# First batch of a fused attention kernel: v loaded ahead of w_out, six of thirteen pieces split, second batch's first keys scored early

## The chip, the cores and the metric

The kernel runs on one core of a Trainium2 chip. The core has five engines with a queue each: PE (TensorE: matrix products into the accumulators, PSUM), DVE (VectorE), ACT (ScalarE), POOL (GpSimd) and SP (SyncE, which here only issues transfers). Each engine takes its instructions strictly in the order in which they were written, so one that waits holds up all behind it. The metric is device time in microseconds (us); a lower one is better. All positions below, such as "at 62.38", are us from the start of the profiled span.

## The reference, cut to what matters

```python
def _attn_ref(q, k, v, agents):            # 4 batches, 12480 tokens, 128 channels, 49 agents
    def sm(a, b):
        s = (a @ b.transpose(0, 2, 1)) / sqrt(128)
        e = np.exp(s - s.max(-1, keepdims=True))
        return e / (e.sum(-1, keepdims=True) + 1e-09)
    agent_v = sm(agents, k) @ v            # needs all keys and values of the batch
    return sm(q, agents) @ agent_v

x = _attn_ref(...).reshape(49920, 128)
out = np.maximum(x @ w_in, 0.0) ** 2 @ w_out       # 128 -> 2048 -> 128
```

w_in and w_out arrive as 64-bit floats and are turned into 32-bit floats on the chip, bit by bit.

## The kernel before

Tokens are cut into 52 groups of 960, thirteen to a batch; keys and values of a batch come in thirteen pieces as well. A batch needs, ahead of its first tokens, its agent values, folded into the first weight matrix (`w_make`: 98 rows of products, a high and a low part, of which 49 rows of `w_lo` are spread over the partitions by small transfers into `w_a` and `w_b`). Once that is there, a group is sixteen steps of: `mm1` (two steps at a time), `relu` and `square` on ACT, `high` and `low` on DVE (a number is split into a rounded high part and the rest, so that PE can take both at its fast 32-bit rate), and `mm2`, four steps later, in the same order on PE (`LAG = 4`). While one batch runs, the next one's keys, values and weights are made in the gaps by a planner (`plan_batch`, `plan_tokens`, `chain`), which hands out one slot per step and engine.

For the first batch nothing runs in which to hide that, so the first 100 us are a preamble written out by hand: a list of `at(time, function)` calls, sorted by time, sets the order on every queue. Its parts, in order:

- keys (`k_load`, `k_scores`, `k_copy`, `k_pmax`) with the conversion of three of the four parts of w_in (`win_make`, seven DVE instructions each) in between, then the maximum over keys (`k_max`, steps 0 to 5, a ping-pong of DVE and PE);
- the v stage, for each of thirteen pieces: `sub0` on DVE, `k_exp` on ACT, then `v_acc_whole` on PE: eight products of 32-bit operands that are not split, accumulated in one PSUM bank over all pieces. Between them on DVE stand the fourth part of w_in and three of the four parts of w_out (`wo_make`, seven instructions each, then `wo_split` on ACT and POOL);
- `v_sum_whole`, `a_final` (PE and DVE by turns), `w_make` for columns 0 and 1 of four, the fourth `wo_make`, and the first steps. The other two `w_make` follow among them; `mm1` of steps 8 and 9 is the first to need the third.

Transfers stand on SP in the order of their `at` times: v piece by piece with a part of w_out after every third and the second group's q after the tenth. Keys, queries and v share a pool of six buffers (`io`), so that a transfer starts when an earlier tile has been read; the raw parts of w_in and w_out have four buffers of another pool (`ew`). Two of the four spread transfers of the first `w_b` are issued by ACT, the others by SP.

Of the kernel before, what the change touches and what calls it, by code (L numbers as in the profile page):

```python
# [25 lines left out]
def agent_attention_relu2_kernel(ctx: ExitStack, tc: tile.TileContext, qT, kT, v, agT, w_in, w_out, outT):  # L26
# [41 lines left out]

    raws = {}

    def raw_load(t, src):
        raw = ew.tile([P, PW, 2], U32, name="raw", tag="gl")
# [29 lines left out]

    def wo_make(t, step):
        if step == 0:
            wo[t] = ew.tile([P, PW], F32, name="wo_f", tag="gh")
            cv["o"] = to_f32(raws.pop((t, False)), wo[t])
        cv["o"][step]()

    def wo_split(t, step):
# [30 lines left out]

    def piece(n):
        return sk[:, n * G:(n + 1) * G, :]
# [50 lines left out]
            nc.sync.dma_start(out=vts[n][:, halves[h]], in_=v[b, :, n * G + h * H:n * G + (h + 1) * H, :])  # L195

    def v_hi(n, h):
        nc.scalar.copy(vss[n % 2][:, halves[h], :C], vts[n][:, halves[h], :C])

    def v_lo(n, h, eng=nc.vector):  # L200
        vs = vss[n % 2][:, halves[h]]
        eng.tensor_tensor(out=vs[:, :, C + 2:], in0=vts[n][:, halves[h], :C], in1=vs[:, :, :C].bitcast(F32), op=ALU.subtract)  # L202

    def v_acc(n):
        vs, pe = vss[n % 2], pes.pop(n)
        vts.pop(n)
        pss["v", n] = bank()
        for c in range(G):
            nc.tensor.matmul(pss["v", n][:A2, :VW], pe[:, c, :], vs[:, c], start=c == 0, stop=c == G - 1)  # L209

    def v_acc_whole(n, ps):

        vt = vts.pop(n)
        for c in range(G):
            nc.tensor.matmul(ps[:A, :C + 1], piece(n)[:, c, :], vt[:, c, :C + 1], start=n == 0 and c == 0, stop=c == G - 1 and n == NS - 1)

    def v_sum_whole(ps):
        nc.vector.tensor_copy(acc[:A, :C + 1], ps[:A, :C + 1])

    def v_sum(n):  # L220
        ps = pss.pop(("v", n))[:A2, :VW]
        if n == 0:
            nc.vector.tensor_copy(acc, ps)
        else:
            nc.vector.tensor_tensor(acc, ps, acc, op=ALU.add)
# [235 lines left out]
    def plan_batch(b, base, span):  # L461

        d = (span - 46) / (2 * NS)
        for n in range(NS):
            t = n if b == 1 and n < AHEAD else base + int(n * d)
            first, end = chain(t, [("PE", k_scores, b, n), ("ACT", k_copy, n), ("DVE", k_pmax, n)])
            if b > 1 or n >= AHEAD:
                at(max(base, first - 8), k_load, b, n)
# [35 lines left out]
    at(Z + .2, q_load, 0)  # L504
    for n in range(NS):
        at(Z + .3 + n * .01, v_load, 0, n)
    at(Z + .395, q_load, 1)
    for n, x, src in ((0, .025, wi_bits), (1, .055, wi_bits), (2, .085, wi_bits), (3, .125, wi_bits),
                      (0, .325, wo_bits), (1, .355, wo_bits), (2, .385, wo_bits), (3, .415, wo_bits)):
        at(Z + x, raw_load, n, src)  # L510
    for n in range(NS):
        t = Z + 6 + KP * n
        at(t, k_scores, 0, n)
# [2 lines left out]
        at(t + 1.8, k_pmax, n)  # L516
    for x in range(7):
        for n in range(3):
            at(Z + 10 + 6 * n + .8 * x, win_make, n, x)
    t0 = Z + 6 + KP * NS  # L520
    at(t0, k_max, 0)
    for x in range(1, 6):
        at(t0 + .8 + .4 * x, k_max, x)
    at(t0 + .1, warm_up, 3)
# [6 lines left out]
    def sub0(n):  # L531
        k_sub(n, nc.vector, pss["m"][:CH, :A])

    for n in range(NS):
        t = t0 + 1.84 * n
        at(t, sub0, n)
        at(t + .5, k_exp, n)
        at(t + 2.4, v_acc_whole, n, vps)
    for x in range(7):
        at(t0 + 2 + .7 * x, win_make, 3, x)  # L540
        for n in range(3):
            at(t0 + 7 + 5 * n + .7 * x, wo_make, n, x)
    for n in range(3):
        for x in range(2):
            at(t0 + 13 + 5 * n + x, wo_split, n, x)
    for x, f in enumerate((q_exp, q_sum, q_inverse, q_norm, q_hi, q_lo)):
        at(t0 + 2 * x + 2.2, f, 0)
    at(t0 + 18, q_transpose, 0)
    for x in range(2):
        at(t0 + 18.1, q_copy, 0, x)  # L550
    at(t0 + 19, q_spread, 0)
    for n in range(AHEAD):
        at(t0 + 20 + .1 * n, k_load, 1, n)
    t += 4.2
    at(t, v_sum_whole, vps)
    at(t + .2, warm_up, 2)
    for x in range(4):
        at(t + .3 + (0, 1, 2, 2)[x], a_final, x)
    at(t + 1.5, warm_up, 4)
    for f in range(2):  # L560
        for x in range(4):
            at(t + 4 + .1 * x + .5 * f, w_make, 0, f, x)
    at(t + 5, warm_up, 3)
# [54 lines left out]
```

## Time and profile before

| | us |
|---|---|
| median of 3 runs | 2052.86 (2051.44 to 2054.33) |
| profiled execution, own time | 2051.45 |
| its span | 2049.7 |
| PE busy of it | 2028.1 (99%) |
| DVE, ACT, POOL busy | 1823.4, 1730.2, 230.8 |

The span is 1.75 us shorter than the execution's own time, and that execution is 1.4 us below the median. PE is busy in nearly all of it, but a share of the span says little here, since the change touches only the first 130 us. Those are read piece by piece: the chain of waits, the order in time of each engine, and narrow windows with the granted clock.

### The profile page before, as it was taken

The numbers are of one execution on the slowest core, as the hardware profiler recorded it, in microseconds if no ns is written. First come the engines' busy times: TensorE is split into PE (matmuls) and PEld (weight loads), VectorE is DVE, ScalarE is ACT, GpSimd is POOL, SyncE is SP. The second block draws the span as 40 slices with busy tenths as digits, with TensorE's granted clock in tenths as the row PEclk, the third lists the DMA queues.
The fourth block names the chain that finished last, engine by engine and source line by source line (L and its number), as shares of the span: only waits on it lengthen the run. The fifth ranks groups of instructions, "written<-read, shape, count | busy, mean of one in ns | idle before, by whom it ended". The sixth has DMA issues, their size and how long they took to land.

```text
span 2049.7 us, 30393 instructions
## 1 busy us (share of the span) xinstructions
PE 2028.1 (99%) x11010; PEld 1584.9 (77%) x11015; DVE 1823.4 (89%) x2274; ACT 1730.2 (84%) x2166; POOL 230.8 (11%) x196
## 2 busy tenths in 40 slices
PE   9899999999999999999999999999999999999999
PEld 8678877777778877777777878777777777777777
DVE  7678899999888889999998888999998888989897
ACT  2488889899888888999888888999888888889897
POOL 0100002221000001232100000122210000000000
PEclk9899999999999999999999999999999999999999
DMA  9322212211121212222112121122111111101010
GB/s 310 90 67 66 71 48 70 79 49 40 56 66 57 66 61 70 61 68 60 35 46 79 56 72 60 61 68 70 45 36 50 44 31 45 30 30 41 29 35 25
DMA packets 51446, 125.16 MB, mean 61 GB/s; under 512 B 7072, under 2 KB 16560, under 8 KB 51296
## 3 DMA queue, kind: packets, MB, share of 16 engines
q1 hardware_dynamic: 51198, 123.19, 19.4%
q8 instruction: 86, 1.41, 0.3%
q14 instruction: 64, 0.52, 0.1%
q10 hardware_dynamic: 98, 0.04, 0.0%
HBM read 81.37 MB, written 25.56 MB: 52 GB/s over the span
## 4 chain that ended last, share of the span: by engine, by line
PE 86%; DVE 8%; issue 4%; DMA 1%; ACT 1%; SPq 0%; ACTq 0%; DVEq 0%
PE out L378 51%; PE h L348 16%; PE h L351 8%; PE ps_att L154 3%; PE ps_att L285 3%; DVE gh L363 3%; DVE gl L367 2%; PE ps_att L322 1%; PE ps_att L209 1%; DVE vs L202 1%; DMA vt<-v 1%; PE ps_att L262 1%; PE h L154 0%; DVE ob L396 0%; PE out L495 0%
## 5 line engine op out<-in xcount | busy, mean ns | idle before, releaser
L367 DVE TENSOR_TENSOR gl<-g,gh 128x960 fp32r<-128x960 f32 x832 | 1015.8, 1221 | 30.6
L355 ACT ACTIVATE r<-h 128x960 f32<-128x960 f32 x832 | 764.4, 974 | 179.0 <-PE h L351 175.8
L359 ACT ACTIVATE g<-r 128x960 f32<-128x960 f32 x832 | 825.5, 1016 | 5.1 <-DVE gl L367 5.1
L378 PE MATMUL out<-gh,wo_hi 128*128 128x480 f32 x1664 | 689.6, 414 | 5.2 <-DVE ob L396 3.6
L363 DVE CAST gh<-g 128x960 fp32r<-128x960 f32 x832 | 583.1, 701 | 99.2 <-ACT g L359 88.0
L378 PE MATMUL out<-gl,wo_hi 128*128 128x480 f32 x1664 | 633.3, 381 | 1.4 <-DVE gl L367 1.1
L378 PE MATMUL out<-gh,wo_lo 128*128 128x480 f32 x1664 | 515.8, 381 | 0.0
L348 PE MATMUL h<-p_a,w_a 126*128 126x480 f32 x1664 | 436.7, 384 | 3.2 <-DMA w_b<-w_lo 2.2
L378 PEld LDWEIGHTS out<-gh,wo_hi 128*128 128x128 f32 x1664 | 313.0, 188 | 141.1 <-issue 71.6
L348 PEld LDWEIGHTS h<-p_a,w_a 126*128 126x128 f32 x1664 | 310.1, 189 | 54.9 <-issue 4.9
L378 PEld LDWEIGHTS out<-gh,wo_lo 128*128 128x128 f32 x1664 | 312.6, 188 | 49.3
L378 PEld LDWEIGHTS out<-gl,wo_hi 128*128 128x128 f32 x1664 | 313.7, 188 | 41.6 <-DVE gl L367 5.7
L351 PE MATMUL h<-p_b,w_b 21*128 21x480 f32 x1664 | 205.4, 479 | 0.7 <-DMA w_b<-w_lo 0.7
L308 POOL TENSOR_TENSOR e<-e,sm 120x392 f32<-120x392 f32 x52 | 55.1, 1060 | 1331.1 <-DVE sm L305 1179.8
L351 PEld LDWEIGHTS h<-p_b,w_b 21*128 21x128 f32 x1664 | 80.2, 182 | 139.9 <-issue 138.1
L285 PEld LDWEIGHTS ps_att<-ag_sb,qt 128*120 128x120 f32 x832 | 96.8, 187 | 3.5
L285 PE MATMUL ps_att<-ag_sb,qt 128*120 128x49 f32 x832 | 94.3, 267 | 0.0
L154 PEld LDWEIGHTS ps_att<-ag_sb,kt 128*120 128x120 f32 x720 | 83.9, 188 | 3.2 <-issue 0.4
L154 PE MATMUL ps_att<-ag_sb,kt 128*120 128x49 f32 x720 | 81.8, 267 | 0.1
L190 POOL TENSOR_TENSOR pe<-sk,pe 120x392 fp32r<-120x392 f32 x39 | 52.9, 1358 | 234.9 <-ACT pe L187 193.0
L158 ACT COPY sk<-ps_att 120x392 f32<-120x392 f32 x45 | 21.9, 487 | 64.8 <-PE ps_att L154 64.8
L315 POOL TENSOR_TENSOR pp<-e,pp 120x392 fp32r<-120x392 f32 x52 | 55.9, 1074 | 161.5 <-ACT pp L312 157.2
(93 smaller groups left out, 936.1 us busy)
## 6 DMA issues: line engine op xcount, KB each, us to landing
vt<-v SPq DMA_DIRECT2D x104, 243.8 KB
kt<-kT SPq DMA_DIRECT2D x52, 480.0 KB
qt<-qT SPq DMA_DIRECT2D x52, 480.0 KB
outT<-ob SPq DMA_DIRECT2D x51, 480.0 KB
p_b<-p_a SPq DMA_DIRECT2D x208, 39.4 KB
p_a<-p_a SPq DMA_DIRECT2D x52, 105.0 KB
raw<-w_in SPq DMA_DIRECT2D x4, 512.0 KB
raw<-w_out SPq DMA_DIRECT2D x4, 512.0 KB
```

The source lines that it names most:

```text
L154: nc.tensor.matmul(ps[:CH, c * A:(c + 1) * A], kt[:, c, :], ag_sb[:, b, :], start=True, stop=True)
L190: eng.tensor_tensor(out=pes[n][:, :, A:], in0=piece(n), in1=pes[n][:, :, :A].bitcast(F32), op=ALU.subtract)
L285: nc.tensor.matmul(ps[:CH, c * A:(c + 1) * A], qt[:, c * CH:(c + 1) * CH], ag_sb[:, s // NS, :], start=True, stop=True)
L308: eng.tensor_tensor(out=es[s], in0=es[s], in1=sms.pop(s).to_broadcast([CH, G, A]), op=ALU.mult)
L315: eng.tensor_tensor(out=pps[s][:, :, A:], in0=es.pop(s), in1=pps[s][:, :, :A].bitcast(F32), op=ALU.subtract)
L348: nc.tensor.matmul(hs[x][:, t, :TT], wa[:K, (x % NF) * P:(x % NF + 1) * P], pa[:K, t, :], start=True, stop=False)
L351: nc.tensor.matmul(hs[i + r // 2][:, r % 2, :TT], wb[rows, i % NF // 2, :], pb[rows], start=False, stop=True)
L355: nc.scalar.activation(rs_[i], hs.pop(i)[:, :, :TT], AF.Relu)
L359: nc.scalar.activation(gs[i], rs_.pop(i), AF.Square)
L363: nc.vector.tensor_copy(ghs[i], gs[i])
L367: nc.vector.tensor_tensor(out=gls[i], in0=gs.pop(i), in1=ghs[i].bitcast(F32), op=ALU.subtract)
L378: nc.tensor.matmul(o[t][:, :TT], w[:, j, :], x[:, t, :], start=st, stop=sp)
```

## The change

- On SP all of v stands ahead of w_out but for one part of w_out ahead of the last two v pieces; then q, a part of w_out, the second batch's first three keys (formerly issued after the v stage), and two more parts of w_out, which lie in `io` now.
- Pieces 0, 2, 4, 6, 9 and 12 are split in the first batch too: `v_hi` and `k_hi` on ACT, `v_lo` and `k_lo` on DVE, eight fast products into the same bank (`v_acc`), 98 rows by 258 columns. The other seven stay whole. `v_sum` copies the full 98 by 258 once.
- No part of w_out is converted in the v stage any more. Two follow the first two `w_make` (ahead of the first step), the third is put into steps 1 to 7, one instruction a step, and the fourth into the planner from step 8.
- `k_scores`, `k_copy`, `k_pmax` of the second batch's pieces 0 to 2 follow the first two `w_make` directly, and are gone from the planner.
- One `win_make` step stands between `k_max` 1 and 3.

```diff
     for n in range(NS):
-        t = t0 + 1.84 * n
         at(t, sub0, n)
         at(t + .5, k_exp, n)
-        at(t + 2.4, v_acc_whole, n, vps)
+        if n in split_n:
+            at(t + 1, k_hi, n)
+            at(t + 1.5, k_lo, n, nc.vector)
+            for h in range(2):
+                at(t - 2 + .5 * h, v_hi, n, h)
+                at(t - 1.5 + .5 * h, v_lo, n, h)
+            at(t + 2.4, v_acc, n, vps, n == split_n[-1])
+            t += 1
+        else:
+            at(t + 2.4, v_acc_whole, n, vps)
+            t += 1.8
...
+    for n in range(AHEAD):
+        at(t + 5 + .1 * n, k_scores, 1, n)
+        at(t + 5.5 + .1 * n, k_copy, n)
+        at(t + 5.5 + .1 * n, k_pmax, n)
     for x in range(7):
-        at(t + 5.5 + .1 * x, wo_make, 3, x)
+        at(t + 6 + .1 * x, wo_make, 0, x)
+        at(t + 8 + .1 * x, wo_make, 1, x)
+        at(1.52 + x, wo_make, 2, x)
     for x in range(2):
-        at(t + 6.5 + x, wo_split, 3, x)
-    at(t + 9, begin)
+        at(t + 7 + x, wo_split, 0, x)
+        at(t + 9 + x, wo_split, 1, x)
+        at(8.52 + x, wo_split, 2, x)
+    at(t + 12, begin)
...
+    chain(8, [("DVE", wo_make, 3, x) for x in range(7)] + [("ACT", wo_split, 3, 0), ("POOL", wo_split, 3, 1)])
```

The queue of SP from the first q on, before (vt is a half of a v piece, raw a part of w_out, p_a and p_b the spread queries):

```order
L279 DMA qt<-qT 128x960
L195 DMA vt<-v 120x520 x6
L78 DMA raw<-w_out 128x4x256
L195 DMA vt<-v 120x520 x6
L78 DMA raw<-w_out 128x4x256
L195 DMA vt<-v 120x520 x6
L78 DMA raw<-w_out 128x4x256
L195 DMA vt<-v 120x520 x2
L279 DMA qt<-qT 128x960
L195 DMA vt<-v 120x520 x4
L78 DMA raw<-w_out 128x4x256
L195 DMA vt<-v 120x520 x2
```

The same place on SP now:

```order
L286 DMA qt<-qT 128x960
L202 DMA vt<-v 120x520 x22
L78 DMA raw<-w_out 128x4x256
L202 DMA vt<-v 120x520 x4
L286 DMA qt<-qT 128x960
L78 DMA raw<-w_out 128x4x256
L155 DMA kt<-kT 128x960 x3
L78 DMA raw<-w_out 128x4x256 x2
L336 DMA p_a<-p_a 28x960
L338 DMA p_b<-p_a 21x480 x4
```

Three parts of w_out and the second q moved behind the last piece of v; keys and two parts of w_out moved ahead of the spread queries.

The end of the v stage on DVE, before (L180 is `sub0`, the raw and cv rows are `wo_make`, L218 reads the finished sum):

```order
L92 SCALAR_TENSOR_TENSOR cv_p<-raw,cv_p 128x512
L93 TENSOR_SCALAR cv_x<-raw 128x512
L180 TENSOR_TENSOR sk<-sk,h 120x392
L94 SCALAR_TENSOR_TENSOR cv_x<-raw,cv_x 128x512
L95 SCALAR_TENSOR_TENSOR wo_f<-cv_x,cv_p 128x512
L180 TENSOR_TENSOR sk<-sk,h 120x392
L218 COPY acc<-out_107 49x129
```

The same place on DVE now (L187 is `sub0`, L209 `v_lo`, L197 `k_lo`, L230 reads the sum):

```order
L187 TENSOR_TENSOR sk<-sk,h 120x392
L209 TENSOR_TENSOR vs_85<-vt,vs_85 120x4x128 x2
L96 SCALAR_TENSOR_TENSOR win_sb<-cv_x,cv_p 128x512
L187 TENSOR_TENSOR sk<-sk,h 120x392 x2
L197 TENSOR_TENSOR pe<-sk,pe 120x8x49
L187 TENSOR_TENSOR sk<-sk,h 120x392
L209 TENSOR_TENSOR vs_86<-vt,vs_86 120x4x128 x2
L187 TENSOR_TENSOR sk<-sk,h 120x392
L197 TENSOR_TENSOR pe<-sk,pe 120x8x49
L230 COPY acc<-out_106 98x258
```

The low halves took the places of the conversions; the two of the last piece stand ahead of its `sub0`.

ACT between the first `w_make` and the first steps, before (w_a is the high part of `w_make`, the DMA rows the two spread transfers, wo_hi the first half of `wo_split`, L355 `relu` of steps 0 and 1):

```order
L264 CAST w_a<-ps_att 98x512
L272 DMA w_b<-w_lo 21x2x128 x2
L264 CAST w_a<-h 98x512
L116 CAST wo_hi<-wo_f 128x512
L355 ACTIVATE r<-h 128x960 x2
```

The same place on ACT now:

```order
L271 CAST w_a<-ps_att 98x512
L279 DMA w_b<-w_lo 21x2x128 x2
L271 CAST w_a<-h 98x512
L165 COPY sk<-ps_att 120x392
L165 COPY sk<-h 120x392
L165 COPY sk<-ps_att 120x392
L118 CAST wo_hi<-wo_f 128x512 x2
L362 ACTIVATE r<-h 128x960 x2
```

Three score copies and a second cast of w_out came in ahead of the first `relu`.

## Rows read from the trace of the kernel before

**Rows 1.** Chain of waits that ended last: start, us, what.

```profile
52.15 10.09 DMA vt<-v
62.38 2.35 PE out L215 x16
...
101.14 0.65 PE h L351
```

**Rows 2.** Order in time, SP's queue: start, us, engine, line, transfer.

```profile
22.50 4.45 SPq L195 DMA_DIRECT2D vt<-v  x6
...
52.15 1.33 SPq L195 DMA_DIRECT2D vt<-v  x2
```

**Rows 3.** Narrow windows of the transfers: granted clock, DMA share, GB/s.

```profile
25.00:26.00 1.00, 1.00 1.04 248
61.00:62.00 1.00, 1.00 0.56 151
```

**Rows 4.** Order in time, DVE, end of keys and v stage.

```profile
32.01 0.21 DVE L167 TENSOR_TENSOR m<-m,pm 120x49 f32<-120x49 f32 x1
...
33.64 0.55 DVE L180 TENSOR_TENSOR sk<-sk,h 120x392 f32<-120x392 f32 x1
...
36.40 0.55 DVE L180 TENSOR_TENSOR sk<-sk,h 120x392 f32<-120x392 f32 x1
36.87 0.42 DVE L89 TENSOR_SCALAR cv_p<-raw 128x512 uint32<-128x512 uint32 x1
...
58.56 0.56 DVE L180 TENSOR_TENSOR sk<-sk,h 120x392 f32<-120x392 f32 x1
```

**Rows 5.** Groups by line and shape, 28 to 60 us: busy us, mean ns.

```profile
L180 DVE TENSOR_TENSOR sk<-sk,h 120x392 f32<-120x392 f32 x13 | 7.2, 554 | 0.0
L183 ACT ACTIVATE sk<-sk 120x392 f32<-120x392 f32 x13 | 6.9, 531 | 17.4 <-DVE sk L180 17.4
```

**Rows 6.** One line's instructions over the whole span: duration ns min/median/max.

```profile
L202 DVE TENSOR_TENSOR vs<-vt,vs x78: 676/684/1465, 297.5 to 1498.4; 120x512 fp32r<-120x512 f32 x78
L198 ACT CAST vs<-vt x78: 612/632/692, 295.8 to 1487.6; 120x512 fp32r<-120x512 f32 x78
L187 ACT CAST pe<-sk x39: 515/535/556, 310.6 to 1495.8; 120x392 fp32r<-120x392 f32 x39
L161 DVE TENSOR_REDUCE pm<-ps_att x45: 553/566/570, 10.2 to 1277.9; 120x49 f32<-120x392 f32 x45
```

**Rows 7.** Order in time, PE: a split piece, later, and a key piece.

```profile
320.04 1.11 PE L209 MATMUL ps_att<-vs,pe 120*98 120x258 f32 x8
...
114.71 1.78 PE L154 MATMUL ps_att<-ag_sb,kt 128*120 128x49 f32 x16
```

**Rows 8.** Order in time, from the end of the v stage to step 0.

```profile
64.77 0.29 DVE L218 COPY acc<-out 49x129 f32<-49x129 f32 x1 [5.65 <-PE out L215]
...
73.37 0.68 DVE L266 TENSOR_TENSOR w_lo<-h,w_a 49x512 fp32r<-49x512 f32 x1 [3.18 <-ACT w_a L264]
...
77.93 0.62 ACT L116 CAST wo_hi<-wo_f 128x512 fp32r<-128x512 f32 x1 [4.59 <-DVE wo_f L95]
78.45 1.82 ACT L355 ACTIVATE r<-h 128x960 f32<-128x960 f32 x2
...
81.59 0.66 DVE L363 CAST gh<-g 128x960 fp32r<-128x960 f32 x1 [0.33 <-ACT g L359]
```

**Rows 9.** Order in time: a DVE conversion beside a POOL instruction.

```profile
54.61 1.27 POOL L118 TENSOR_TENSOR wo_lo<-wo_f,wo_hi 128x512 fp32r<-128x512 f32 x1 [4.90 <-ACT wo_hi L116]
...
55.10 1.32 DVE L92 SCALAR_TENSOR_TENSOR cv_p<-raw,cv_p 128x512 uint32<-128x512 uint32 x1
...
75.34 0.69 DVE L92 SCALAR_TENSOR_TENSOR cv_p<-raw,cv_p 128x512 uint32<-128x512 uint32 x1
```

**Rows 10.** Narrow windows of PE: busy us, granted clock (1.00 is 2.4 GHz).

```profile
74.00:75.00 1.00, 0.90 (x2) 0.50 0.00 0
...
102.00:103.00 1.00, 1.00 (x3) 0.50 0.08 22
```

More of the change, by code (lines that the diff above doesn't have):

```diff
@@ L69, in agent_attention_relu2_kernel, with raw_load @@
     raws = {}
-    def raw_load(t, src):
-        raw = ew.tile([P, PW, 2], U32, name="raw", tag="gl")
+    def raw_load(t, src, late=False):
+        raw = (io if late else ew).tile([P, PW, 2], U32, name="raw", tag="io" if late else "gl")
         raws[t, src is wi_bits] = raw
@@ L106, in wo_make @@
         if step == 0:
-            wo[t] = ew.tile([P, PW], F32, name="wo_f", tag="gh")
-            cv["o"] = to_f32(raws.pop((t, False)), wo[t])
+            late = t > 1
+            wo[t] = (io if late else ew).tile([P, PW], F32, name="wo_f", tag="io" if late else "gh")
+            cv["o"] = to_f32(raws.pop((t, False)), wo[t], late)
         cv["o"][step]()
@@ L132, in agent_attention_relu2_kernel, with slot @@
     kts, vts, pes, pss = {}, {}, {}, {}
+    slots = {}
+    def slot(n):
+        return slots.get(n, n) % 2
     many = [True]
@@ L197, in v_hi, with v_acc @@
     def v_hi(n, h):
-        nc.scalar.copy(vss[n % 2][:, halves[h], :C], vts[n][:, halves[h], :C])
+        nc.scalar.copy(vss[slot(n)][:, halves[h], :C], vts[n][:, halves[h], :C])
     def v_lo(n, h, eng=nc.vector):
-        vs = vss[n % 2][:, halves[h]]
+        vs = vss[slot(n)][:, halves[h]]
         eng.tensor_tensor(out=vs[:, :, C + 2:], in0=vts[n][:, halves[h], :C], in1=vs[:, :, :C].bitcast(F32), op=ALU.subtract)
-    def v_acc(n):
-        vs, pe = vss[n % 2], pes.pop(n)
+    def v_acc(n, ps=None, last=True):
+        vs, pe = vss[slot(n)], pes.pop(n)
         vts.pop(n)
-        pss["v", n] = bank()
+        if ps is None:
+            pss["v", n] = bank()
+        out = (ps if ps is not None else pss["v", n])[:A2, :VW]
         for c in range(G):
-            nc.tensor.matmul(pss["v", n][:A2, :VW], pe[:, c, :], vs[:, c], start=c == 0, stop=c == G - 1)
+            nc.tensor.matmul(out, pe[:, c, :], vs[:, c], start=c == 0 and (ps is None or n == 0), stop=c == G - 1 and last)
     def v_acc_whole(n, ps):
@@ L214, in v_acc_whole, with v_sum @@
         for c in range(G):
[L215 to L222, printed above, removed]
+            nc.tensor.matmul(ps[:A, :C + 1], piece(n)[:, c, :], vt[:, c, :C + 1], start=False, stop=False)
+    def v_sum(n, ps=None):
+        whole = ps is not None
+        ps = (ps if whole else pss.pop(("v", n)))[:A2, :VW]
+        if n == 0 or whole:
             nc.vector.tensor_copy(acc, ps)
@@ L464, in plan_batch @@
         for n in range(NS):
[L465 to L468, printed above, removed]
+            if b == 1 and n < AHEAD:
+                continue
+            first, end = chain(base + int(n * d), [("PE", k_scores, b, n), ("ACT", k_copy, n), ("DVE", k_pmax, n)])
+            at(max(base, first - 8), k_load, b, n)
             if n == NS - 2:
@@ L498, in begin @@
         many[0] = False
+        slots.clear()
     Z, KP = -100.0, 1.9
@@ L532, in sub0 @@
         k_sub(n, nc.vector, pss["m"][:CH, :A])
+    t = t0
+    split_n = (0, 2, 4, 6, 9, NS - 1)
+    slots.update((n, x) for x, n in enumerate(split_n))
     for n in range(NS):
-        t = t0 + 1.84 * n
         at(t, sub0, n)
         at(t + .5, k_exp, n)
-        at(t + 2.4, v_acc_whole, n, vps)
-    for x in range(7):
[L540 to L545, printed above, removed]
+        if n in split_n:
[9 more added lines that the diff above has]
+            t += 1.8
+    for x in range(7):
+        at(t0 + 4 + 1.4 * x, win_make, 3, x)
     for x, f in enumerate((q_exp, q_sum, q_inverse, q_norm, q_hi, q_lo)):
         at(t0 + 2 * x + 2.2, f, 0)
-    at(t0 + 18, q_transpose, 0)
+    at(t0 + 14.1, q_transpose, 0)
     for x in range(2):
[L550 to L556, printed above, removed]
+        at(t0 + 14.2, q_copy, 0, x)
+    at(t0 + 15, q_spread, 0)
+    t += 2.4
+    at(t, v_sum, NS - 1, vps)
+    at(t + .2, warm_up, 3)
     for x in range(4):
         at(t + .3 + (0, 1, 2, 2)[x], a_final, x)
-    at(t + 1.5, warm_up, 4)
+    at(t + 1.5, warm_up, 6)
     for f in range(2):
@@ L562, in agent_attention_relu2_kernel @@
             at(t + 4 + .1 * x + .5 * f, w_make, 0, f, x)
-    at(t + 5, warm_up, 3)
+    for n in range(AHEAD):
+        at(t + 5 + .1 * n, k_scores, 1, n)
+        at(t + 5.5 + .1 * n, k_copy, n)
+        at(t + 5.5 + .1 * n, k_pmax, n)
     for x in range(7):
-        at(t + 5.5 + .1 * x, wo_make, 3, x)
+        at(t + 6 + .1 * x, wo_make, 0, x)
+        at(t + 8 + .1 * x, wo_make, 1, x)
+        at(1.52 + x, wo_make, 2, x)
     for x in range(2):
-        at(t + 6.5 + x, wo_split, 3, x)
-    at(t + 9, begin)
+        at(t + 7 + x, wo_split, 0, x)
+        at(t + 9 + x, wo_split, 1, x)
+        at(8.52 + x, wo_split, 2, x)
+    at(t + 12, begin)
     plan_tokens(1, 1, True)
```

21 lines of the change are left out of this document (12 added, 9 removed).

## Prediction

> **What bounds the kernel now.** The table says PE busy 99%, so from the first steady step to the last output PE sets the pace. The change removes next to nothing from that stretch, so the question is when it begins. I therefore read first the chain of waits through the preamble [rows 1]: at its end of the v stage stands a transfer of v, issued at 52.15 [rows 2] and waited for until 62.38; then the last piece on PE takes 2.35, so the v stage ends at 64.73. DVE had finished its last subtraction at 59.12 [rows 4]. So the v stage is bound by loading, by about 3 us against what DVE would have allowed. The transfers run full at 248 GB/s [rows 3] nearly to the end; at 61 to 62 the share falls to 0.56.
>
> From 64.73 on the order in time shows a serial chain [rows 8]: the sum is read at 64.77, the second w_lo ends at 74.05, one part of w_out is converted on DVE and cast on ACT at 77.93, relu of step 0 at 78.45, and `high` of step 0, from which DVE's work on the steps runs, at 81.59. PE waits for that chain, it doesn't set it. The last point is the end of `mm1` of steps 8 and 9 at 101.79 [rows 1], which waited for the third part of the spread weights; from there PE has no wait worth naming. I take that as the point to compare: **what moves 101.79 moves the end**, and PE work taken from behind it comes off too.
>
> **The v stage.** Ahead of the last piece of v stood four parts of w_out and a q, 4 x 0.524 + 0.492 = 2.59 MB; one part remains. At 248 GB/s [rows 3] the 2.06 MB are 8.3 us, so the last piece could land at 62.38 - 8.3 = 54.1, if six buffers come free fast enough; I take 54.6.
>
> That doesn't end the stage, since six pieces now need DVE and ACT. Start: the maximum's first half ends at 32.22 [rows 4]; a low half of v (0.68, the median of [rows 6]) and a conversion (0.69, [rows 9]) now stand ahead of the next reduce, which used to begin 0.45 later. So subtractions begin 0.9 later, 33.64 + 0.9 = 34.5. To the end of the last but one item DVE then has: 12 subtractions x 0.554 [rows 5] = 6.6; 10 further low halves of v x 0.68 = 6.8; 5 low halves of the scores, the same shape as the subtraction, x 0.554 = 2.8; three instructions of the first queries like the reduce of [rows 6], 1.7; two small ones, 0.4; seven of w_in, which I read from [rows 8]: 74.05 to 77.93 = 3.9. Sum 22.2, so 56.7. Rows overlap a little (a row of 0.55 at 36.40, the next at 36.87, [rows 4]): some 0.08 x 38 = 3.0 come off. Against that every low half waits for its cast on ACT (0.63 or 0.54, [rows 6]), and ACT has 12 casts of v, 6 of scores and 13 exponentials of 0.53 [rows 5], 7.6 + 3.2 + 6.9 = 17.7 in the same 23 us, in a fixed order. The neighbours are the bounds: 53.7 without any such wait, 60 if half of the 12 casts are waited for in full. Going through both orders row by row I get 57.5 for the start of the last subtraction. Then, in series: subtraction 0.55, exponential 0.53, cast 0.54, low half 0.55, eight products 1.11 [rows 7], 3.3 together. **End of the v stage 60.8**, 3.9 ahead of 64.73. The PE time that split products save (1.11, [rows 7], for the 2.35 of [rows 1], part of which ran at half clock) is worth nothing: PE is not waited for there.
>
> **From there to step 0.** Before: 81.59 - 64.73 = 16.9 us. All of that chain stays, and ACT's order now puts two casts of w_out ahead of relu of step 0. DVE therefore has, between the second w_lo and the last cast, three key maxima (3 x 0.566 = 1.7, [rows 6]) and two conversions for one: + 3.9. The POOL half of the first split falls into the second conversion. A DVE step beside such a POOL instruction took 1.32 for 0.69 [rows 9], so + 0.6. Back: a score copy (0.5, like the cast of the same shape in [rows 6]) formerly stood between relu and square. Together + 5.7, so `high` of step 0 comes 22.6 after the end of the v stage, at **83.4, 1.8 later than before**. The score products themselves (3 x 1.78, [rows 7]) lie in PE's wait for the spread weights and cost nothing; nor do they gain there, since PE is not what this chain waits for.
>
> The Trainium skill ("SBUF — State Buffer", section "Who interferes with whom") says that a DVE instruction with two inputs in SBUF, or a tensor_scalar in its two-port form, and a reading GpSimd instruction exclude one another for the whole instruction. By that the loser waits up to the 1.27 of the POOL row, and the sum would be 0.6 higher; the row pair showed about half of it, and the row decides.
>
> **From step 0 to the end of mm1 8 and 9.** Before 101.79 - 81.59 = 20.2. On DVE four conversion steps (0.42 to 0.69 each, [rows 4, 9], 2.0 together) come in ahead of the third w_lo, but DVE had waited there for square of step 2 about as long, since mm1 of step 2 ran at half the clock (0.50 from 74 on, [rows 10]). Hidden wholly they add nothing, not at all 2.0. I take 19.9, the first end, less 0.3 for `mm1` being earlier relative to `high`. So 83.4 + 19.9 = 103.3, **1.5 later**.
>
> **Behind it.** Before, two of the three early key pieces had run ahead of that point and one behind it, at 114.71, 1.78 us of PE [rows 7]: **- 1.8**. In the stretch ahead of the point PE has less to do than before, since a key piece that stood there is gone, and waits longer; the clock was at half at 102 to 103 already after a shorter wait [rows 10]. Each further us at half clock costs half a us; I add **+ 1.0** for two more such us (0 to 3, for none to six). DVE has eleven more conversion steps behind the point, 6 us, against slack: I add **+ 0.3** (0 to 4).
>
> Sum: + 1.5 - 1.8 + 1.0 + 0.3 = **+ 1.0**. Against the profiled execution's 2051.45 that is 2052.5; the median lies 1.4 above it, so on the median's scale 2052.86 + 1.0 = **2053.9**. A measurement of this kernel can tell about 0.2%, 4.1 us, from no change; this is none.
>
> **Rivals.** (a) *DVE keeps up with the loads*: no wait for casts, the last subtraction at 53.7, but the last piece landing at 54.1 and needing two casts and two low halves (1.9), then 3.3: v stage at 58 to 59, 2 to 3 earlier than I say; and the clock back as soon as before: - 1.0. That gives 2050, and 2048 if the POOL overlap and DVE's backlog are nothing as well. For it: DVE's durations alone. Against: the fixed order of two engines that wait for one another 18 times.
>
> (b) *The last piece lands late, and is split.* It is followed now by casts, low halves, subtraction, exponential and the rest, 1.9 + 3.3 = 5.2 us from landing to the end of the stage, where a whole piece needed 2.35. Six buffers bound how early it is asked for: each of its forerunners must be read first, and those that stay whole are read only when PE has used them. If it lands later than 55.6, each us goes through one for one; landing at 60, 4.4 later, makes 2058.3, slower. For it: in the trace a v transfer asked for at 52.15 was waited for until 62.38, ten us. Against: eight us of that were others' bytes.
>
> (c) *DVE becomes the bound of the first group.* Fifteen conversion steps, 8 us, beside sixteen steps of `high` and `low`; if half of it is not absorbed, + 4: 2057.9. Against: behind step 8 `mm2` follows `low` by several steps.
>
> (d) *It doesn't do what it says*: the loads don't come earlier because buffers stay full; then the stage ends as before or, by (b), later; it is in (b).
>
> **How the numbers follow.** Forecast 0.58; (a) 0.18, of which a good half has the further terms too, so 0.10 faster and 0.08 same; (b) 0.14, 0.12 of it slower; (c) 0.10, 0.07 slower; the rest of both is same. From the forecast's own spread (v stage 1.5 either way, the added terms 0 to 7) 0.04 go to faster and 0.03 to slower. Faster 0.14, same 0.64, slower 0.22. The range leaves out a tenth at either end: 2048.8 to 2058.8.
>
> **What would show it.** In the profile after: the last v transfer lands near 55 and PE's last v product ends near 61 (near 59: a; near 65: b); DVE's second conversion of w_out ends some 19 us after that and relu of step 0 right behind it; `high` of step 0 near 83; the last of `mm1` 8 and 9 near 103, with PE waiting some 5 us ahead of it and at half clock behind it; no key product of the second batch near 115. If relu of step 0 starts well ahead of the second cast, or PE has long waits between 105 and 130, the sum is wrong in its second or last part.

## The result, and the profile after

The changed kernel takes 2060.53 us (median of 5 runs, 2057.87 to 2063.02); the kernel before, timed beside it, 2052.37 (2050.96 to 2054.33). The ratio is 1.0038, with a 95% interval from 1.0023 to 1.0053: slower by 8.2 us, outside the forecast range. A second set of runs of the same kernel (`e11_changed_again` below) gave 1.0039 [1.0026, 1.0053]. A profile shows one execution, which can lie up to 4.4 us from the median of its kernel's runs (`e9_one_in_v`: 2045.54 for 2049.89), so times below are medians and stretches are those of the profiled execution.

The profiled execution took 2060.53 with a span of 2058.7, 9.0 longer than the span before. Its page says that PE is under nine tenths busy in the first two of its 40 slices (51 us each) alone, and the granted clock under nine tenths in the third (lines of the page: PE's busy share and PE's clock, in tenths by slice):

```profile
PE   8799999999999999999999999999999999999999
...
PEclk9989999999999999999999999999999999999999
```

So I cut the preamble at five points that every kernel here has: the first key product on PE, DVE's first subtraction, the read of the sum of v, `high` of step 0, and the end of `mm1` of steps 8 and 9. A sixth point is a steady one behind the first steps, the transposes of group 2 (groups count from 0), a seventh the transposes of a late group. In the trace of after, order in time on DVE and PE (start, us, engine, line, operation, tiles, idle time ahead and its releaser), these rows mark them; they answer to [rows 1, 4, 8]:

```profile
62.79 0.43 DVE L230 COPY acc<-out 98x258 f32<-98x258 f32 x1 [1.29 <-PE out L218]
85.50 0.66 DVE L370 CAST gh<-g 128x960 fp32r<-128x960 f32 x1 [3.31 <-ACT g L366]
103.59 1.57 PE L358 MATMUL h<-p_b,w_b 21*128 21x480 f32 x2 [0.33 <-DMA w_b<-w_lo]
156.55 0.82 PE L329 MATMUL ps_att<-ident_r,pp 120*98 120x120 f32 x8
```

The same transposes in the order in time of the kernel before:

```profile
148.88 0.83 PE L322 MATMUL ps_att<-ident_r,pp 120*98 120x120 f32 x8
```

The distances between these points, in us, for the two kernels, for the second profile of after, and for what the forecast's steps say (each is the distance before plus the step's change):

| stretch | before | forecast | after | after, second profile |
|---|---|---|---|---|
| first key product to first subtraction | 27.63 | 28.5 | 28.52 | 28.52 |
| first subtraction to read of the sum (v stage) | 31.13 | 26.3 | 28.86 | 30.69 |
| to `high` of step 0 | 16.82 | 22.5 | 22.71 | 22.72 |
| to end of `mm1` 8 and 9 | 20.20 | 19.9 | 19.66 | 19.66 |
| to transposes of group 2 | 47.09 | 46.6 | 51.39 | 48.90 |
| to transposes of a late group | 1778.11 | 1778.1 | 1779.27 | 1779.33 |

Three rows came out as worked out, to 0.3 us. The excess is in the other three: v stage +2.5 and +4.4, the first steps behind step 8 +4.8 and +2.3, and 1.2 spread over the long rest.

**The v stage** begins at half clock. PE waits 1.71 us for DVE's first step of the keys' maximum; the clock falls to 1.2 GHz (0.50), and the first queries' sixteen products take 3.43. DVE has the maximum over these products in its queue, ahead of low halves of v and of the scores, and waits 2.21 for them. Order in time of after, PE and DVE, then narrow windows (busy us and count of PE, PEld, DVE, ACT, POOL, granted clock, DMA share, GB/s):

```profile
31.77 0.37 PE L177 MATMUL ps_att<-ident,m 120*49 120x120 f32 x1 [1.71 <-DVE m L174]
...
33.70 3.43 PE L292 MATMUL ps_att<-ag_sb,qt 128*120 128x49 f32 x16
37.16 0.57 DVE L297 TENSOR_REDUCE mx<-ps_att 120x8 f32<-120x392 f32 x1 [2.21 <-PE ps_att L292]
38.86 2.04 PE L218 MATMUL out<-vs,pe 120*98 120x258 f32 x8 [1.73 <-DVE pe L197]
```

```profile
31.00:32.00 1.00, 0.23 (x2) 0.21 (x3) 0.97 (x3) 0.00 (x0) 0.00 (x0) 0.91 1.01 252
32.00:33.00 1.00, 1.00 (x3) 0.09 (x1) 1.00 (x4) 0.00 (x0) 0.00 (x0) 0.50 1.00 252
```

The wait is not new, though. The kernel before has it too, 1.70 us long and empty of PE work, and there the clock stayed up. Order in time on PE and a window of the kernel before:

```profile
32.36 0.28 PE L170 MATMUL ps_att<-ident,m 120*49 120x120 f32 x1 [1.70 <-DVE m L167]
...
31.00:32.00 1.00, 0.00 (x0) 0.00 (x0) 0.97 (x1) 0.00 (x0) 0.00 (x0) 1.00 1.03 243
```

The low half of v and the conversion that now stand in the keys' maximum come behind the step that PE waits for. So no run shows that the change brought the clock down there: of the eleven profiles with these five fillers, all with a wait of 1.7, seven have the fall behind it and four (`before` among them) do not.

In this profile no row of the last pieces waits for a transfer, as PE did in [rows 1]; they wait for the other engine. Order in time on DVE at the end of the stage:

```profile
58.02 1.29 DVE L209 TENSOR_TENSOR vs<-vt,vs 120x512 fp32r<-120x512 f32 x2 [1.59 <-ACT vs L205]
...
60.93 0.57 DVE L197 TENSOR_TENSOR pe<-sk,pe 120x392 fp32r<-120x392 f32 x1 [1.15 <-ACT pe L194]
```

It was close: the last half of v was asked for at 50.7 and landed at 57.5 by the trace's transfer records, 0.3 ahead of its cast. In the second profile of the same program it was asked for at 51.2 and landed at 59.6, and there ACT's cast waited for it. Order in time of that profile, ACT:

```profile
59.66 0.62 ACT L205 CAST vs<-vt 120x512 fp32r<-120x512 f32 x1 [1.55 <-DMA vt<-v]
```

What made that transfer slower was not looked into.

**Behind step 8** stands a wait that the forecast did not have. `mm2` of step 12 is the first to read the fourth part of w_out. Its seven conversion steps lie among DVE's `high` and `low` of steps 8 to 14; the last ends at 124.27; then ACT casts it, POOL makes the low part in 2.15, and PE waits for both. Order in time on DVE, ACT, POOL and PE, and a window behind it:

```profile
123.59 0.68 DVE L96 SCALAR_TENSOR_TENSOR wo_f<-cv_x,cv_p 128x512 f32<-128x512 f32 x1
124.30 0.62 ACT L118 CAST wo_hi<-wo_f 128x512 fp32r<-128x512 f32 x1 [0.91 <-DVE wo_f L96]
125.00 2.15 POOL L120 TENSOR_TENSOR wo_lo<-wo_f,wo_hi 128x512 fp32r<-128x512 f32 x1 [16.67 <-ACT wo_hi L118]
124.98 0.49 PE L385 MATMUL out<-gh,wo_hi 128*128 128x480 f32 x1 [0.30 <-ACT wo_hi L118]
127.21 1.03 PE L385 MATMUL out<-gh,wo_lo 128*128 128x480 f32 x2 [1.09 <-POOL wo_lo L120]
128.04 3.28 PE L292 MATMUL ps_att<-ag_sb,qt 128*120 128x49 f32 x16
```

```profile
126.00:127.00 1.00, 0.12 (x1) 0.00 (x0) 1.00 (x2) 1.00 (x2) 1.00 (x1) 1.00 0.03 8
...
128.00:129.00 1.00, 1.00 (x7) 0.96 (x5) 0.87 (x1) 1.00 (x2) 0.00 (x0) 0.50 0.00 0
```

After one us with PE busy for 0.12 of it the clock is at 0.50 until 134, and the sixteen products take 3.28 where such a set took 1.78 [rows 7].

### The profile page after: what moved, and what is told of

It is laid out like the page before. It is cut to its first block, busy times and chain, and to the rows that moved or that the text cites. A ratio compares the mean times of both kernels' runs of the same rounds, so it can differ in the third digit from the quotient of the medians.

```text
span 2058.7 us, 30345 instructions
## 1 busy us (share of the span) xinstructions
PE 2029.4 (99%) x10967; PEld 1582.3 (77%) x10967; DVE 1833.9 (89%) x2291; ACT 1738.5 (84%) x2184; POOL 232.2 (11%) x196
## 4 chain that ended last, share of the span: by engine, by line
PE 86%; DVE 8%; issue 4%; ACT 1%; DMA 0%; POOL 0%; SPq 0%; DVEq 0%; ACTq 0%
PE out L385 51%; PE h L355 16%; PE h L358 8%; PE ps_att L161 3%; PE ps_att L292 3%; DVE gh L370 3%; DVE gl L374 2%; PE ps_att L329 2%; PE ps_att L218 1%; DVE vs L209 1%; PE h L161 1%; PE ps_att L269 1%; DVE ob L403 0%; ACT g L366 0%; PE out L501 0%
## 5 line engine op out<-in xcount | busy, mean ns | idle before, releaser
L355 PE MATMUL h<-p_a,w_a 126*128 126x480 f32 x1664 | 438.1, 385 | 11.1 <-ACT r L362 8.0
L355 PEld LDWEIGHTS h<-p_a,w_a 126*128 126x128 f32 x1664 | 310.4, 189 | 64.7 <-ACT r L362 9.3
L197 POOL TENSOR_TENSOR pe<-sk,pe 120x392 fp32r<-120x392 f32 x39 | 52.6, 1349 | 235.2 <-ACT pe L194 193.3
```

The lines of the kernel that those rows point to most:

```text
L197: eng.tensor_tensor(out=pes[n][:, :, A:], in0=piece(n), in1=pes[n][:, :, :A].bitcast(F32), op=ALU.subtract)
L355: nc.tensor.matmul(hs[x][:, t, :TT], wa[:K, (x % NF) * P:(x % NF + 1) * P], pa[:K, t, :], start=True, stop=False)
```

## The experiments

The theory after the first profile: several separate places, each with its price, and all of them come from putting conversions of w_out behind the v stage and splitting pieces in it. The rivals differ by experiment. Times are medians; all ratios are to the kernel before on the same chip, with 95% intervals.

**The fourth part earlier.** Its steps keep their slots in the planner as empty calls, and are done at steps 8 to 12.

```
-    chain(8, [("DVE", wo_make, 3, x) for x in range(7)] + [...])
+    for x in range(7):
+        at(8.6 + .5 * x, wo_make, 3, x)
+    for x in range(2):
+        at(12.1 + .05 * x, wo_split, 3, x)
```

> The changed kernel with the fourth part of w_out converted in steps 8.6 to 11.6, two instructions a step, instead of steps 8 to 14 (planner's slots kept). Theory: mm2 of step 12 waited there for that part's low half, from about 125 to 127.2, and the clock was at half from 127.7 to 134.9; without the wait 2.2 and half of 7 come back, 5.8 together: about 2055 where the changed kernel takes 2060.5. Rival, DVE is the bound of the first group: two conversions a step make high and low later, PE waits for those instead, and the time stays within 1.5 of 2060.5 or gets longer.

Measured 2057.77, 1.0031 [1.0019, 1.0043]. The low part starts on POOL 5.2 earlier and PE waits for it no more; no half clock follows. Order in time of this kernel, POOL:

```profile
119.80 2.17 POOL L120 TENSOR_TENSOR wo_lo<-wo_f,wo_hi 128x512 fp32r<-128x512 f32 x1 [10.68 <-ACT wo_hi L118]
```

The stretch behind `mm1` 8 and 9 fell from 51.39 (48.90 in the second profile) to 47.77. So the wait is real, and 1.1 to 3.6 us is its price with its clock; the 5.8 expected was too much. It is no clean price, since the half clock that begins ahead of this point reaches 6.0 us past it here and 5.1 in after. Nor do the times settle it alone: the intervals of this kernel and of after overlap, and that the rival (DVE as the bound) is not what happened is read from the trace, in which PE has no wait over 0.3 us there.

**More fillers while the keys' maximum is built.**

```
-    at(t0 + .1, warm_up, 3)
-    at(t0 + 1.7, warm_up, 2)
+    at(t0 + .1, warm_up, 8)
+    at(t0 + 1.7, warm_up, 4)
```

> The changed kernel with 12 filler products instead of 5 while DVE takes the maximum over keys. Theory: PE's empty time at 30 to 33 let the clock fall to half until 42, which made the query scores 1.6 longer and the v stage end 1.5 to 2 later than counted; with fillers the clock stays at full, the v stage ends near 61 and the time falls by about 1.5. Rival, the v stage is paced by DVE and ACT: its end stays at 62.6 within 0.4 and the time within 1.

Measured 2057.6, 1.0031 [1.002, 1.0042], with runs from 2054.57 to 2061.27, of which the profiled one took 2055.44. In it PE waited 0.64 in place of 1.71, the clock stayed at 2.4 GHz, the first queries took 1.88, DVE waited 0.66 for them in place of 2.21, and the v stage took 27.30. Those 1.55 us are the whole difference to the 28.86 of after. Order in time of this kernel, PE and DVE:

```profile
32.12 0.28 PE L177 MATMUL ps_att<-ident,m 120*49 120x120 f32 x1 [0.64 <-DVE m L174]
...
33.81 1.88 PE L292 MATMUL ps_att<-ag_sb,qt 128*120 128x49 f32 x16
35.73 0.57 DVE L297 TENSOR_REDUCE mx<-ps_att 120x8 f32<-120x392 f32 x1 [0.66 <-PE ps_att L292]
...
125.21 0.70 PE L385 MATMUL out<-gh,wo_lo 128*128 128x480 f32 x2 [1.10 <-POOL wo_lo L120]
125.75 1.78 PE L292 MATMUL ps_att<-ag_sb,qt 128*120 128x49 f32 x16
```

The last two rows are as instructive: the wait for the fourth part is there, of the same length, but the clock did not fall behind it. The same wait is followed by half clock in one trace and not in another.

**The three key pieces back in the planner**, where they were before.

```
-    for n in range(AHEAD):
-        at(t + 5 + .1 * n, k_scores, 1, n)
-        at(t + 5.5 + .1 * n, k_copy, n)
-        at(t + 5.5 + .1 * n, k_pmax, n)
```

> The changed kernel with the second batch's first three key pieces scored in steps 0 to 2 by the planner again (their loads stay early). Theory: early scoring moves 1.8 of PE work from behind the wait for the third weights, and puts 1.7 of maxima ahead of step 0, so it is worth nothing: 2060.5 within 2. Rival, it holds PE's clock up and fills its wait: without it 4 or more longer.

Measured 2058.44, 1.0034 [1.0022, 1.0046], 2.1 under the expected 2060.5, so just outside its 2. The way to `high` of step 0 is 21.32 in place of 22.71: the three maxima cost 1.4 there (the forecast had 1.7). And PE does not wait at step 12 at all: POOL's low part took 1.28 here, not 2.15, and ended at 124.58, 0.3 ahead of its reader, with no half clock behind it. So the wait in after is a near thing; whether the key piece of 1.78 that stands on PE ahead of step 12 again or the shorter POOL instruction removed it was not separated. Order in time of this kernel, POOL, then PE:

```profile
123.30 1.28 POOL L120 TENSOR_TENSOR wo_lo<-wo_f,wo_hi 128x512 fp32r<-128x512 f32 x1 [16.39 <-ACT wo_hi L118]
124.91 0.60 PE L385 MATMUL out<-gh,wo_lo 128*128 128x480 f32 x2
```

**No piece split.**

```
-    split_n = (0, 2, 4, 6, 9, NS - 1)
+    split_n = ()
```

(The sum and its start and stop flags follow, as in the kernel before.)

> The changed kernel with all thirteen pieces of v whole. Theory: PE isn't what the v stage waits for, but DVE and ACT with 18 casts and low halves; whole, it ends when PE has done 13 x 1.97 from 36 on, or 2.4 behind the last landing: 60 to 61.5 instead of 62.6, the time 1 to 2.5 shorter. Rival, the split saves what it is meant to, 0.8 for each of six pieces: the stage ends 3 or more later without it.

Measured 2056.04, 1.0019 [1.001, 1.0028]. The v stage takes 26.35, the shortest of all: PE has two runs of 96 products without a gap, and DVE is empty for 13 us at its end. Order in time of this kernel, PE, then DVE:

```profile
37.36 10.81 PE L224 MATMUL out<-vt,sk 120*49 120x129 f32 x96 [0.39 <-ACT sk L190]
...
48.93 10.80 PE L224 MATMUL out<-vt,sk 120*49 120x129 f32 x96
59.78 0.28 DVE L230 COPY acc<-out 49x129 f32<-49x129 f32 x1 [13.00 <-PE out L224]
```

So loading v first, with the conversions of w_out out of the way, is worth 31.13 - 26.35 = 4.8 of v stage (with one conversion put back, in the last two experiments, it is still 26.35), and the split gives none of it: eight split products save 0.77 on PE (1.97 for sixteen whole ones, 1.20), but with casts, low halves and their waits the stage is 1.0 longer with the clock up (27.30), and 2.5 to 4.3 longer in the profiles in which the clock fell.

**The first two cures together.**

> The changed kernel with both cures at once: the fourth part of w_out converted at steps 8 to 12 (as in e1_part4_early) and twelve fillers in place of five while the keys' maximum is built (as in e2_warm_kmax). Theory (the loss is two separate places, the half clock that the empty TensorE of the keys' maximum brings on and the wait of step 12 for the fourth part): the gains of the two, 2.8 and 2.9 us, add, and the time is about 2060.5 - 5.7 = 2054.8, within 2053.5 to 2056, close to the blind forecast; v stage ends near 61.5, mm1 of steps 8 and 9 ends near 103.7, no wait of TensorE over 0.5 us between 106 and 130. Rival (the two gains are the same half clock, which either cure only moves): 2057 to 2058, as with each alone.

Measured 2056.11, 1.0018 [1.001, 1.0027], 0.1 above the theory's range and 0.9 under the rival's: 0.0020 under after, where the two alone gave 0.0007 each, with intervals that overlap. Behind step 8 the stretch is 46.41, against 46.6 forecast: with the fourth part early nothing of that miss is left. This prices the wait apart from the clock. The half clock in this stretch lasted 3.0 us here, 3.9 with the fillers alone, 6.0 with the fourth part alone, 6.6 in the second profile of after and 12.0 in its first. The fillers alone have the wait and 47.64, 1.2 more than here, of which 0.9 us more at half clock explain half, 0.45; the wait is left with 0.8. Half of the extra half clock, and 0.8 where the wait stands, then make +1.5, +2.6 and +5.3 for the other three, which measured +1.4, +2.5 and +5.0. The fillers, however, did not hold the clock this time. It fell at 37, out of the wait of 1.74 for the first low half of the scores, which `e2_warm_kmax` has as well, without a fall. The v stage was 28.96; ACT's cast of the last v half waited 1.55 for its transfer here too. Narrow windows of this kernel, columns as above:

```profile
36.00:37.00 1.00, 0.42 (x5) 0.30 (x3) 0.54 (x2) 1.00 (x3) 0.00 (x0) 1.00 0.87 287
37.00:38.00 1.00, 0.00 (x0) 0.00 (x0) 1.00 (x3) 0.77 (x2) 0.00 (x0) 0.71 1.07 208
```

So the gain of the fillers alone is not shown to be theirs. That the half clock makes a split v stage 1.6 longer is shown, by the queries' products; the 1.7 here and the 3.4 of the second profile stand beside a late transfer as well.

**Conversions on the DVE that the unsplit v stage leaves empty.** From `e4_no_split`, parts 0 and 1 go there:

```
-        at(t + 6 + .1 * x, wo_make, 0, x)
-        at(t + 8 + .1 * x, wo_make, 1, x)
+        at(t0 + 22.1 + .05 * x, wo_make, 0, x)
+        at(t0 + 23 + .05 * x, wo_make, 1, x)
```

(and their splits with them.)

> As e4_no_split (no piece is split), and the first two parts of w_out are converted at the end of the v stage, where VectorE stood empty for 13.0 us, and no conversion is left between the v stage and step 0; nothing else is moved. Theory (the conversions ahead of step 0 set it): the 11.7 us between the end of the keys' weights and the first high part shrink to what the weights' rows take, so the first high part starts 4 to 6 us earlier than the 82.4 of e4_no_split, at 76.5 to 78.5; the wait of step 12 for the fourth part stays, so the time falls by 3 to 6 us from 2056.0, to 2050 to 2053. Rival 1 (the spread rows of the weights or the second part's late load are as late anyway): high part at 81 to 82, time 2055 to 2056. Rival 2 (the time comes back at step 12, since the third and fourth part's conversion is bound by their load and by VectorE's steps, not by step 0): high part near 77, but the eight transposes of the second group move by less than half of that.

Measured 2051.32, 0.9995 [0.9986, 1.0004]. The way from the sum to `high` of step 0 fell from 22.63 to 15.05, 7.6 us for two conversions. But the second part's words came late, and the read of the sum is queued behind its steps on DVE. Order in time of this kernel, DVE:

```profile
56.03 0.43 DVE L90 TENSOR_SCALAR cv_p<-raw 128x512 uint32<-128x512 uint32 x1 [7.02 <-DMA raw<-w_out]
...
62.36 0.43 DVE L90 TENSOR_SCALAR cv_p<-raw 128x512 uint32<-128x512 uint32 x1 [2.46 <-DMA raw<-w_out]
...
66.14 0.28 DVE L230 COPY acc<-out 49x129 f32<-49x129 f32 x1
```

The stage grew to 32.03, and `high` came at 81.19, 1.2 earlier and not the 4 to 6 expected. That the time still fell by the 3 to 6 expected is luck: most of it, 3.6 us, came behind step 8, where the same 1.1 us wait of step 12 as in `e4_no_split` was not followed by half clock.

**That, the fourth part early, and all four pieces of the keys' weights ahead of step 0** (pieces 2 and 3 keep empty calls in the planner).

```
+    for f in range(2, F // 512):
+        for x in range(4):
+            at(t + 5.8 + .1 * x + .5 * (f - 2), w_make, 0, f, x)
```

> As e6_convert_in_v, with the fourth part converted at steps 8 to 12 (as in e1_part4_early) and all four pieces of the keys' weights made ahead of step 0, so that step 8 finds the third. Theory (waits at step 0, step 8 and step 12 are three separate prices): 2 to 5 us under e6_convert_in_v, 2047 to 2050, and so under the kernel before; no wait of TensorE over 0.6 us between the first steps and 130. Rival (the pieces made earlier lengthen the way to step 0 by what they save at step 8): within 1 us of e6_convert_in_v less 2.5.

Measured 2050.99, 0.9995 [0.9986, 1.0004]: no gain. The wait of step 8 went, but the cast of the fourth part on ACT stood ahead of a relu and held it. Order in time of this kernel, ACT, then PE:

```profile
111.08 0.62 ACT L118 CAST wo_hi<-wo_f 128x512 fp32r<-128x512 f32 x1 [4.22 <-DVE wo_f L96]
111.61 1.82 ACT L364 ACTIVATE r<-h 128x960 f32<-128x960 f32 x2
112.62 2.03 PE L357 MATMUL h<-p_a,w_a 126*128 126x480 f32 x4 [3.93 <-ACT r L364]
```

**The kernel before with all four weight pieces early.**

```
-    for f in range(2):
+    for f in range(F // 512):
         for x in range(4):
             at(t + 4 + .1 * x + .5 * f, w_make, 0, f, x)
```

> The kernel before with all four pieces of the keys' weights made ahead of step 0, nothing else changed; it prices the wait of step 8 for the third piece, which both kernels have (2.4 us of empty TensorE and then 3.0 us at half clock in the kernel before). Theory: 2 to 4 us under the kernel before, 2048.5 to 2050.5. Rival (the two further pieces lengthen the way to step 0 by as much): the same as before within 1 us.

Measured 2050.7, 0.9994 [0.9985, 1.0003], not told from no change (1.8 us under the kernel before on its chip). In its trace `high` of step 0 comes 0.9 later after the sum, and from there to the transposes it is 64.36 for 67.29: 2.0 net, at the lower end of the theory.

**One conversion in the unsplit v stage, one behind it, the fourth part early with its cast after step 14**, without and with the early weight pieces (as in `e7_all_three`). From `e4_no_split`:

```
-        at(t + 6 + .1 * x, wo_make, 0, x)
+        at(t0 + 22.1 + .05 * x, wo_make, 0, x)
...
-        at(t + 7 + x, wo_split, 0, x)
+        at(t0 + 22.5 + .05 * x, wo_split, 0, x)
...
+        at(8.6 + .5 * x, wo_make, 3, x)
...
+        at(14.1 + .05 * x, wo_split, 3, x)
```

> As e4_no_split (no piece split), with one conversion (the first part of w_out) at the end of the v stage, whose raw words landed at 56.0 in e6_convert_in_v, one left between the v stage and step 0, and the fourth part converted at steps 8 to 12, its copy on ScalarE after step 14 so that no later relu is queued behind it (the 3.93 us of e7_all_three). Theory (each wait has its own price): the sum of the keys is copied at about 60, the first high part starts near 76 to 78 (16 to 17.5 us later, as in the kernel before), no wait for the fourth part; 3 to 5 us under e6_convert_in_v, 2046 to 2049, under the kernel before too. Rival (what stands between the v stage and step 0 is set by the spread of the weights' rows and the fillers, and step 8's piece takes the rest back): 2050 to 2053.

> As e9_one_in_v, with all four pieces of the keys' weights made ahead of step 0. Theory: the wait of step 8 for the third piece goes, 1.5 to 3 us under e9_one_in_v, 2044 to 2047. Rival (the two pieces lengthen the way to step 0): within 1 us of e9_one_in_v.

Measured 2049.89, 0.9985 [0.9976, 0.9994], and 2046.71, 0.9974 [0.9964, 0.9984]. The second is as expected, 5 us under the kernel before, and so faster than both. In its profiled execution, the quickest of its runs at 2043.32, the v stage is 26.35 again, the sum is read at 59.85, and behind `mm1` of steps 4 and 5 PE has no wait over 0.7 us up to the transposes of group 2. Order in time of this kernel, DVE, then PE:

```profile
59.85 0.29 DVE L230 COPY acc<-out 49x129 f32<-49x129 f32 x1 [3.11 <-PE out L224]
...
79.62 0.66 DVE L372 CAST gh<-g 128x960 fp32r<-128x960 f32 x1 [3.31 <-ACT g L368]
...
81.73 2.03 PE L357 MATMUL h<-p_a,w_a 126*128 126x480 f32 x4 [1.12 <-ACT r L364]
...
111.12 0.48 PE L387 MATMUL out<-gl,wo_hi 128*128 128x480 f32 x1 [0.70 <-DVE gl L376]
```

The first has the wait for the third weight piece still (3.84 at step 8), and at 2049.89 it lies 0.9 above what its theory gave and just under the rival's 2050.

**The changed kernel again.**

> The changed kernel once more, unedited, for a second profile. Theory (the spells at half clock of its first 135 us come from waits that the program has): the same 2.2 to 4 us of half clock after steps 8 and 12, the wait for the fourth part again over 1 us, time 2059 to 2061. Rival (the spells are chance of one execution): the waits again, the spell after step 12 not; the ratio to before closer to 1.002 than to 1.004.

Measured 2059.81, 1.0039 [1.0026, 1.0053]. The same waits at steps 8 and 12 and the same time, but in the v stage the wait for the last transfer (the ACT row at 59.66 above), and other lengths of half clock: 13.6 us of it in the v stage in place of 10.3, and after step 12 some 3.4 us in place of 6.8. The time fits the theory; that each spell comes back at its size does not.

All kernels at the same points, in us (after by its first profile; where the early weight pieces move the third point, the last two stretches are added):

| kernel | v stage | to `high` 0 | to `mm1` 8/9 | to group 2 | late group | ratio |
|---|---|---|---|---|---|---|
| before | 31.13 | 16.82 | 20.20 | 47.09 | 1778.11 | 1 |
| after | 28.86 | 22.71 | 19.66 | 51.39 | 1779.27 | 1.0038 |
| e1 fourth part early | 28.88 | 22.71 | 19.66 | 47.77 | 1779.35 | 1.0031 |
| e2 fillers | 27.30 | 22.72 | 19.67 | 47.64 | 1779.33 | 1.0031 |
| e3 keys back | 28.85 | 21.32 | 19.67 | 48.92 | 1779.40 | 1.0034 |
| e5 e1 and e2 | 28.96 | 22.72 | 19.67 | 46.41 | 1779.39 | 1.0018 |
| e4 no split | 26.35 | 22.63 | 19.67 | 51.54 | 1777.98 | 1.0019 |
| e6 two in v | 32.03 | 15.05 | 19.67 | 47.93 | 1778.05 | 0.9995 |
| e7 that, fourth part, weights | 31.15 | 15.82 | 67.02 | | 1777.93 | 0.9995 |
| e8 before, weights early | 30.80 | 17.74 | 64.36 | | 1778.08 | 0.9994 |
| e9 one in v | 26.35 | 17.85 | 19.67 | 45.65 | 1778.17 | 0.9985 |
| e10 and weights | 26.35 | 19.77 | 61.09 | | 1778.15 | 0.9974 |

## Why the prediction was wrong

**What bounds the kernel.** Right: nothing but the preamble and the first group moved, and the 1.2 us of the long rest. But "from there PE has no wait worth naming", said of the point at 101.79, was read from before and carried to after, where it no longer held.

**The v stage** failed by 2.5 us (4.4 in the second profile). The start of the subtractions was right (0.9 later). From there DVE's sum and the waits between two engines gave 26.3, and with the clock up they took 27.30, 1.0 more. Two terms were put at nothing. PE was left out as "not waited for", but DVE's queue waits for the first queries' products, and at half clock these cost 1.55 more. And the last v piece was taken to land at 54.6, "if six buffers come free fast enough": it landed at 57.5, and at 59.6 in the second profile, where the stage waited for it. The fall of the clock could not be read off the kernel before, where the same wait of PE left it up. Two of the step's own figures do not follow: half of 12 casts waited for makes 53.7 + 6 x 0.63 = 57.5 and not the upper bound of 60, and rival (a)'s 54.1 + 1.9 + 3.3 is 59.3, not 58 to 59.

**From there to step 0** held: +5.7 said, +5.9 measured, also by its parts: maxima 1.4 for 1.7, and e6 prices two conversions at 7.6 together. The POOL overlap was larger than the 0.6 taken. Order in time of after, POOL, then DVE:

```profile
78.14 1.26 POOL L120 TENSOR_TENSOR wo_lo<-wo_f,wo_hi 128x512 fp32r<-128x512 f32 x1 [26.12 <-ACT wo_hi L118]
...
78.24 1.44 DVE L92 TENSOR_SCALAR cv_p<-cv_p 128x512 uint32<-128x512 uint32 x1
```

A step of 0.43 took 1.44, so 1.0 was lost. The row pair of [rows 9] gave 0.6. By the rule of the Trainium skill ("SBUF — State Buffer", section "Who interferes with whom"), of a `tensor_scalar` in its two-port form and a GpSimd instruction the one that comes second waits out the other's whole instruction. This row fits that better: the step began 0.10 after POOL and ended 0.28 after it.

**From step 0 to the end of `mm1` 8 and 9** held: 19.66 for 19.9. The four conversion steps were hidden, as taken.

**Behind it** failed by 4.8 us (2.3 in the second profile): the +0.3 for "eleven conversion steps, 6 us, against slack". The number that was missing is a due time. The steps were weighed against DVE's idle time, where the question was when the fourth part is first read: by `mm2` of step 12, some 125 us in, with cast and POOL's 2.15 still to come after the last step. Its operands came late by 1.4 in all (0.30 and 1.09), which cost some 0.8; the rest is half clock, most of it the 6.8 us behind that wait (3.4 in the second profile). The forecast's own price of the clock, +1.0 for two more us, was meant for step 8, where after has 5.1 us of it behind the point for 2.9 in before. With the fourth part early the stretch is 46.41 for 46.6, so the other terms come out in their sum, but not one by one: e5 has only 3.0 us at half clock there, so the +1.0 in it was not the clock. The -1.8 for the key piece was not measured by itself, and e3 shows that with that piece in its old place step 12 had no wait.

**The rivals.** (b), the last piece lands late and is split, has the right mechanism for the v stage: its 5.2 us from landing to the end, counted from 59.6, make 64.8 where the sum was read at 64.5 in the second profile. Counted from 57.5 they make 62.7, the end in after, though there no row waits for the transfer. (c), DVE as the bound of the first group, came near in the time (2057.9), but by a different road: not `low`, which it weighed, but the operand that DVE makes. (a) fell: the casts were waited for. No rival had the two places together. The last sentence of the forecast, that long waits of PE between 105 and 130 would show the sum wrong in its last part, named one of them, though the wait there was 1.4 and not long.

The terms close: e5, whose clock fell in the v stage but not behind step 12, has +0.9 - 2.2 + 5.9 - 0.5 - 0.7 + 1.3 = +4.7 by its trace (its median says +3.6), and the forecast's +1.0 with 2.6 for the v stage and 1.2 for the long rest is +4.8.

## What to carry to other kernels

For work that is pushed back into "slack", look up when its product is first read and count back from there through every engine that still has to touch it; idle time of the engine that does the work says nothing about that. A load moved ahead can be the whole gain: here splitting pieces to speed an engine that no longer was short of time took 1 to 4 us of it back. The dearest piece to split is the one that lands last, which then needs some 5 us to the end of the stage in place of 2.35; leaving that one alone whole was not tried. And the engine time that a faster stage leaves empty (13 us of DVE here) is the place for the work that the change displaced, provided that its data has landed by then and no later reader is queued behind it.

## What the runs showed of the hardware

The half clock lasts. In the kernel before PE was empty for most of 72 to 74, and then stayed at 1.2 GHz until 87.7 though it was busy for 0.90 or more of every us. Narrow windows of the kernel before, columns as above:

```profile
73.00:74.00 1.00, 0.22 (x2) 0.00 (x0) 0.63 (x2) 0.33 (x1) 0.00 (x0) 0.99 0.16 43
...
75.00:76.00 1.00, 1.00 (x6) 0.39 (x5) 0.97 (x3) 0.00 (x0) 0.00 (x0) 0.50 0.23 57
...
86.00:87.00 1.00, 1.00 (x3) 0.57 (x2) 0.15 (x1) 0.94 (x3) 0.00 (x0) 0.50 0.00 0
```

Spells of 3.4 to 17 us were seen, and whether one follows a short wait, and how long it is, differs between executions: behind the same 1.1 us wait of step 12 there were 6.8 and 3.4 us of it in the two profiles of after, and none in e2's and e6's. Behind the same 1.7 us wait for the keys' maximum the clock fell in seven of eleven profiles, with the old preamble (`e8_before_w_early`) and with the new one.

Left open: every kernel with split pieces takes 1779.3 to 1779.4 us from group 2 to the late group, every one without 1777.9 to 1778.2, though PE has no waits between 1700 and 1900 in either kind. The mean `mm1` product was 380 ns against 378 there. What carries that on was not tried.
